# Induced attention and a maxout layer in one kernel: another list of work, some products in column tiles, another head

## The chip, the cores and the metric

One NeuronCore of a Trainium2 chip runs the whole program. The metric is device time in microseconds (us) of one execution, median of the runs shown. The profile is of one further execution, whose own time stands beside its span below.

## What is computed

```python
def mab(q, kv):                       # scale = 1 / sqrt(128)
    a = softmax(scale * q @ kv.T); return a @ kv
h = mab(inducing, x)                  # x: 4 x 12544 x 128, inducing: 32 x 128
y = mab(x, h)                         # 4 x 12544 x 128
g = maximum(y @ w1, y @ w2)           # w1, w2: 128 x 1024
out = g @ w_out                       # 50176 x 128, f32
```

The kernel uses maximum(a, b) = a + relu(b - a): the ReLU part goes through 1024 hidden columns, the linear part y @ w1 @ w_out through one 128 x 128 matrix. Since y is a weighted sum of the 32 rows of h, y @ (w2 - w1) is e @ (h @ (w2 - w1)), where e are the 32 weights of a token before division by their sum (`hwd` is h @ (w2 - w1), `m1` is h @ w1 @ w_out). The division comes last, when a result leaves PSUM.

## The kernel before

Each batch has 98 chunks of 128 tokens. Chunks stand in 27 blocks of up to 4 quarters x 4 chunks: quarter q of a block has its 32 rows of e on partitions 32q to 32q + 31.

Work on TensorE has three tilings. **Full array**: a final product (L932) has 128 x 128 ReLU values as the stationary operand and streams 128 columns of w_out; 8 of them, and the linear part, make a chunk of output, and up to 4 chunks share a PSUM bank (a group). **Row tiles**, 32 x 128: a phase (L1031, products at L1085) runs up to four quarters side by side, 512 columns each, hwd times e, into a bank for each; with fewer than four quarters the linear part of a group (e times m1, same line) may be one of them. **Column tiles**, 128 x 32: `stage` (L657) makes four quarters' scores, whose exp (ScalarE, L669) is e of a block; `pool_scores` (L356) and `pool_accum` (L414) are the first attention of batches 1 to 3.

A bank of a phase is emptied by ScalarE (L1102) or VectorE (L1105) with a ReLU into the quarter's buffer (two of 4096 columns for each quarter). A finished group is divided on its way out of PSUM by VectorE (L964) or ScalarE (L971), after the digit of its index in `EVICT`, and SP stores it. `turn_e2` (L720, L724) has GpSimd add up e and take the reciprocals.

The order of work in the steady part is a string, `ORDER` (L1113): a number is so many final products; `pN.M` a phase of N quarters; `s` a stage; `c`, `t`, `a`, `r` pooling scores, DMA transpose, sums, rest; `x` a DMA transpose of x; `g` a block's denominators; `e`, `h`, `w`, `m` the small products of a batch; `H`, `W` parts of the weights. The engine of a ReLU is the one that would end first by a planner (`Clock`, L21) that runs beside the program's writing; a bit of M turns that choice over. The planner also fills long waits with idle products (`keep_busy`), and picks banks.

Before that stands the **head**: batch 0 arrives in 12 parts (part 0 by SP in f32, the others by GpSimd's DMA queue, which casts to f16 on the way; L195), then the weights in four pieces (L253, L254) and w_out (L255). Each part is transposed by TensorE in two halves (L276; copied out by VectorE, L280, and ScalarE, L283), gives scores (L292), exp (L305), and the sums of e (L319) and e times x (L328). The order is the string `HEAD` (L814), with the due times of the parts in `LANDED`. At its end: the differences w2 - w1 (L573: 0 to 255 and 256 to 511 by VectorE, 512 to 1023 by GpSimd), casts of w1 (L579 by VectorE, L582 by ScalarE), hT4 (L473), two quarters of hwd (L521, evicted at L525), the first block's e (L684, L696), w1's transposes (L589, L596, L599) and w1 @ w_out (L607). `H1` is hwd's second half, evicted by VectorE, and the second half of the transposes; `W` is L607.

Of the kernel before, what the change touches and what calls it, by code (L numbers as in the profile page):

```python
# [9 lines left out]
F16 = mybir.dt.float16  # L10
# [10 lines left out]
class Clock:  # L21


    PAIR = 0.0558
    SWITCH = {"full": 0.11, "row": 0.097, "col": 0.097}
    LAT = 0.20
    ROW = 0.224
    SEM = 0.05

    def __init__(self):  # L30
        self.pe = self.act = self.dve = self.sp = 0.0
        self.pool = self.loading = self.loaded = 0.0
        self.stored = [0.0] * NOUT
        self.issue, self.tile = 0.0, [0.0] * 4
        self.mode = "full"
        self.bank = [0.0] * 8
        self.idle = {}
        self.log = []
        self.busy = {}
# [7 lines left out]
    def run(self, us, mode="full", ready=0.0, why="data"):  # L47
        if mode != self.mode:
            self.pe += self.SWITCH[mode]
            self.busy["sw"] = self.busy.get("sw", 0) + self.SWITCH[mode]  # L50
# [6 lines left out]
    def on_act(self, ready, us, tail=0.12):  # L57
# [3 lines left out]
    def on_dve(self, ready, us, tail=0.085):  # L61
# [3 lines left out]
    def on_sp(self, ready, us=1.33):  # L65
# [9 lines left out]
        return max(start + us + 2.4, late)  # L75
# [56 lines left out]
def kernel(  # L132
# [28 lines left out]
    relup = ctx.enter_context(tc.tile_pool(name="relup", bufs=2))  # L161
    outp = ctx.enter_context(tc.tile_pool(name="outp", bufs=NOUT))
# [7 lines left out]
    uid = [0]  # L170

    def bank(shape, dtype=F32, only=None):
        i = min(range(8), key=lambda j: ck.bank[j]) if only is None else only
        uid[0] += 1
        return i, psum.tile(shape, dtype, name=f"ps{uid[0]}", tag=f"bank{i}", bufs=1)
# [7 lines left out]
    parts[0] = [(0, 14), (14, 14), (28, 14), (42, 14), (56, 7), (63, 7), (70, 7), (77, 7), (84, 6), (90, 4), (94, 2), (96, 2)]  # L183
# [6 lines left out]
    def load_x(b, i, after=None):  # L190
# [5 lines left out]
        if b:  # L196
# [3 lines left out]
            st[b]["ld", i] = ck.loaded = ck.pe + 8.0 + 2.75 * i if b > 1 else 26.2 + 2.5 * i  # L200
# [13 lines left out]
    head16 = relup.tile([128, 4096], F16, name="head", tag="relu3")  # L214
# [10 lines left out]
    wf = relup.tile([128, 4096], F16, name="wf", tag="relu0").bitcast(F32)  # L225
    w1f, w2f = wf[:, 0:J], wf[:, J : 2 * J]
    w1s = relup.tile([128, 4096], F16, name="w1s", tag="relu1")
# [10 lines left out]
    with tc.manual_schedule(engines={ET.PE, ET.DVE, ET.Activation, ET.Pool, ET.SP}):  # L238

        xf = relup.tile([128, 4096], F16, name="xf", tag="relu2")[:, 0 : 256 * P1].bitcast(F32)  # L240
        xf = xf.rearrange("p (k c) -> p k c", c=C)
# [3 lines left out]
        load_x(0, 1)  # L245
        make_identity(nc, identity16)
        load_x(0, 2)
        make_identity(nc, identity32)
        for i in range(3, len(parts[0])):
            load_x(0, i)  # L250
        for h in range(2):
            sl = slice(512 * h, 512 * (h + 1))
            nc.gpsimd.dma_start(out=w1f[:, sl], in_=moe_w1[:, sl])  # L253
            nc.gpsimd.dma_start(out=w2f[:, sl], in_=moe_w2[:, sl])  # L254
        nc.gpsimd.dma_start(out=woutp, in_=moe_w_out.rearrange("(jb j) c -> j jb c", j=128))  # L255
# [6 lines left out]
        nc.gpsimd.memset(m1bd, 0.0)  # L262
# [3 lines left out]
        LANDED = [0.0, 7.58, 9.72, 11.95, 13.05, 14.12, 16.27, 17.37, 18.31, 18.94, 19.26, 19.57]  # L266

        def p1_transpose(b, i, half):
            k0, n = parts[b][i]
            xn = xn_at[b, i]  # L270
            h = min(8, (n + 2) // 2)
            g, m = ((0, h), (h, n - h))[half]
            assert m
# [3 lines left out]
            end = ck.run(0.0555 * m, ready=max(ck.bank[bi], LANDED[i] + 0.1), why="T")  # L277
            dst = xT_tiles[b % 2][:, k0 + g : k0 + g + m, :]
            if half == 0:
# [7 lines left out]
        def p1_scores(b, i):  # L287
# [12 lines left out]
            if n > 2:  # L300
                et = etp.tile([128, P1, M], F16, name=f"et_{b}_{i}", tag="et")
            else:
                at = 1024 + 2 * M * (i % 2)
                et = head16[:, at : at + 2 * M].rearrange("p (k m) -> p k m", m=M)
            nc.scalar.activation(out=et[:, 0:n, :], in_=ps[:, 0 : n * M], func=AF.Exp, scale=scale)  # L305
            ck.bank[bi] = ck.on_act(end, 0.05 + n * M / 1200.0)
            st[b]["et", i] = et, ck.bank[bi]

        def p1_accum(b, i, lo=0, hi=P1):
# [4 lines left out]
            if b == 0:  # L314
                last = i == len(parts[0]) - 1
                ck.wait(ready, "p1")
                for j in range(lo, hi, 4):
                    m = min(4, hi - j)
                    nc.tensor.matmul(  # L319
                        out=st[0]["eps"][0 : m * M, 0:1],  # L320
                        lhsT=et[:, j : j + m, :].rearrange("p k m -> p (k m)"),
# [880 lines left out]
```

## Time and profile before

| | before |
|---|---|
| median of 3 runs | 318.08 us (318.03 to 318.1) |
| the profiled execution | 317.76 us, its span 316.0 us |
| granted TensorE clock | 0.998 |
| first phase of the steady part | 23.44 us |
| last product of TensorE ends | about 312.9 us |
| DMA | 55.81 MB, mean 177 GB/s |

In the profile PE is TensorE, PEld its loads of stationary operands, DVE VectorE, ACT ScalarE, POOL GpSimd. The span goes from the first to the last instruction. A group of instructions is named by its line, engine, operation and operands, then the count, the busy time (of all, in us), the mean of one in ns, and the idle time before them with what ended it. A wait is written "who <- whom: us in total, times, longest". The chain leads from the last instruction back to what released each; its rows are the start, the us, and what ran. Products on TensorE overlap in the pipeline and their shown ends are modelled, so their pace is the difference of starts.

### The profile page before, as it was taken

What the parts mean: (1) busy time and instruction counts of PE and PEld (TensorE: products, weight loads), DVE (VectorE), ACT (ScalarE), POOL (GpSimd) and SP (SyncE); (2) the same over time, 40 slices, a digit from 0 to 9 for tenths busy, and PEclk for the clock granted to TensorE, in tenths of its full rate; (3) what the DMA queues carried; (4) which work ended last, traced back from release to release, by engine and by line L of the source; (5) the groups of instructions that cost most, each with busy time, mean ns of one, the idle gap of its engine ahead of it and who ended that gap; (6) DMA issues with size and microseconds to landing.
All of it is one profiled execution on the core that took longest, in us unless ns stands there. A gap on an engine that the chain in (4) does not pass through costs nothing.

```text
span 316.0 us, 12577 instructions
## 1 busy us (share of the span) xinstructions
PE 308.6 (98%) x5308; PEld 239.9 (76%) x5308; DVE 274.5 (87%) x488; ACT 280.2 (89%) x580; POOL 125.8 (40%) x187
## 2 busy tenths in 40 slices
PE   6998999999999999999999999999999999999996
PEld 3885777777877777778877787887868777788885
DVE  2468999999878999988999899989899889999885
ACT  3669999999999999998999989899999999998891
POOL 7363060666620066067510064674406564461500
PEclk9999999999999999999999999999999999999999
DMA  8999999989799999898499999897323233324232
GB/s 203 208 252 205 207 219 146 207 229 230 127 218 245 245 183 174 190 233 207 121 225 252 213 227 215 204 174 203 106 85 118 100 106 118 119 88 140 102 120 101
DMA packets 81336, 55.81 MB, mean 177 GB/s; under 512 B 62816, under 2 KB 66176, under 8 KB 81280
## 3 DMA queue, kind: packets, MB, share of 16 engines
q1 hardware_dynamic: 75312, 41.32, 55.8%
q0 software_dynamic: 5968, 13.70, 22.4%
q8 instruction: 41, 0.67, 0.9%
q14 instruction: 15, 0.12, 0.1%
HBM read 27.28 MB, written 25.69 MB: 168 GB/s over the span
## 4 chain that ended last, share of the span: by engine, by line
PE 94%; DMA 2%; ACT 1%; DVE 1%; issue 1%; POOL 0%; POOLq 0%
PE ps L932 60%; PE ps L1085 23%; DMA xn<-in_x_dram 2%; PE ps L657 2%; PE ps L356 2%; PE ps L414 2%; PE ps L276 1%; PE ps L328 1%; PE ps L292 1%; PE ps L521 0%; DVE relu L1105 0%; PE ps L319 0%; ACT e L669 0%; DVE o L964 0%; ACT e_first L696 0%
## 5 line engine op out<-in xcount | busy, mean ns | idle before, releaser
L1102 ACT ACTIVATE relu<-ps 128x512 f16<-128x512 f32 x470 | 241.0, 627 | 17.5 <-PE ps L1085 16.5
L1105 DVE TENSOR_SCALAR relu<-ps 128x512 f16<-128x512 f32 x314 | 199.7, 684 | 20.6 <-PE ps L1085 19.0
L932 PE MATMUL ps<-woutp,relu 128*128 128x128 f16 x3136 | 203.5, 219 | 0.2
L932 PEld LDWEIGHTS <-relu 128*128 128x128 f16 x3136 | 176.6, 98 | 34.4 <-issue 28.7
L1085 PE MATMUL ps<-e,hwd 32*128 32x512 f16 (+2 forms) x840 | 82.8, 361 | 0.1
L720 POOL TENSOR_TENSOR half<-ed 128x256 f32<-128x256 f16 (+2 forms) x23 | 14.1, 613 | 145.8 <-DMA ed<-e 145.8
L724 POOL TENSOR_TENSOR rd<-den,minus 128x16 f32<-128x16 f32 (+2 forms) x23 | 60.7, 2639 | 1.8
L964 DVE TENSOR_TENSOR o<-ps,rd 128x512 f32<-128x512 f32 (+3 forms) x83 | 53.2, 643 | 3.9 <-PE ps L1085 2.8
L1085 PE MATMUL ps<-m,e 32*128 32x128 f16 x372 | 36.8, 216 | 0.0
L1085 PEld LDWEIGHTS <-hwd 32*128 32x128 f16 x880 | 26.7, 91 | 12.8 <-issue 3.8
L1085 PEld LDWEIGHTS <-e 32*128 32x128 f16 x372 | 22.4, 92 | 10.4 <-issue 2.7
L720 POOL TENSOR_TENSOR half<-half 128x32 f32<-128x32 f32 (+3 forms) x69 | 22.3, 323 | 5.4
L195 POOL DMA_DIRECT2D xn<-in_x_dram x32 | 17.6, 563 | 5.7 <-DMA xn<-in_x_dram 4.3
L280 DVE COPY xT<-ps 128x512 f16<-128x512 f16 (+3 forms) x12 | 5.7, 485 | 8.6 <-PE ps L276 8.6
L964 DVE TENSOR_TENSOR o<-ps,rp 128x512 f32<-128x512 f32 (+3 forms) x20 | 12.8, 642 | 0.0
L369 ACT ACTIVATE eu<-ps 128x512 f16<-128x512 f32 x18 | 11.0, 617 | 0.6 <-PE ps L356 0.3
L669 ACT ACTIVATE e<-ps 128x512 f16<-128x512 f32 (+2 forms) x21 | 11.1, 607 | 0.3 <-PE ps L657 0.2
L283 ACT COPY xT<-ps 128x768 f16<-128x768 f16 (+3 forms) x10 | 5.7, 574 | 4.3 <-PE ps L276 4.2
L276 PE MATMUL ps<-identity,xn 128*128 128x128 f16 x98 | 7.6, 220 | 1.4 <-DMA xn<-in_x_dram 0.9
L657 PE MATMUL ps<-xT,hT 128*32 128x512 f16 (+3 forms) x110 | 8.1, 361 | 0.1
L276 PEld LDWEIGHTS <-xn 128*128 128x128 f16 x98 | 5.5, 97 | 2.9 <-DMA xn<-in_x_dram 1.2
L356 PE MATMUL ps<-xT,inducingT 128*32 128x512 f16 x72 | 6.8, 386 | 0.0
(110 smaller groups left out, 117.7 us busy)
## 6 DMA issues: line engine op xcount, KB each, us to landing
out_dram<-o SPq DMA_DIRECT2D x90, 256.0 KB, 3.0
xn<-in_x_dram POOLq DMA_DIRECT2D x24, 448.0 KB, 10.4
out_dram<-o SPq DMA_DIRECT2D x10, 128.0 KB, 2.9
wf<-in_moe_w_dram POOLq DMA_DIRECT2D x4, 256.0 KB, 6.0
xn<-in_x_dram POOLq DMA_DIRECT2D x4, 224.0 KB, 10.2
xT<-xn SPq DMA_TRANSPOSE x33, 4.4
xf<-in_x_dram SPq DMA_DIRECT2D x1, 512.0 KB, 3.7
xf<-in_x_dram SPq DMA_DIRECT2D x1, 384.0 KB, 4.2
```

The source lines that it names most:

```text
L195: nc.gpsimd.dma_start(out=xn_at[b, i][:, 0:n, :], in_=xr[b, :, k0 : k0 + n, :])
L276: nc.tensor.transpose(ps[:, j, :], xn[:, g + j, :], identity16)
L356: nc.tensor.matmul(out=ps[32 * g : 32 * (g + 1), :], lhsT=inducingT, rhs=xT_tiles[b % 2][:, U * u + 4 * g : U * u + 4 * (g + 1), :], start ...
L657: nc.tensor.matmul(out=ps[32 * q : 32 * (q + 1), 128 * t : 128 * (t + n)], lhsT=hq, rhs=xT[:, c : c + n, :], start=True, stop=True, tile_p ...
L669: nc.scalar.activation(out=blk.e2[:, 0 : 128 * wd], in_=ps[:, 0 : 128 * wd], func=AF.Exp, scale=st[0]["rs"] if blk.b == 0 else scale,)
L720: nc.gpsimd.tensor_tensor(out=dst, in0=cur[:, :, 0:n], in1=cur[:, :, n : 2 * n], op=ALU.add)
L724: nc.gpsimd.tensor_tensor(out=rp[:, 0:wd, :].rearrange("p t q -> p (t q)"), in0=den[:, 0 : 4 * wd], in1=minus1[:, 0 : 4 * wd], op=ALU.pow,)
L932: nc.tensor.matmul(out=g.ps[:, 128 * c : 128 * (c + 1)], lhsT=g.blk.relu[g.q][:, 128 * (jb * w4 + t) : 128 * (jb * w4 + t + 1)], rhs=woutp ...
L964: nc.vector.tensor_mul(osb[:, 0:m, :], g.ps[:, 0 : m * C].rearrange("p (s c) -> p s c", s=m), g.blk.rp[:, t0 : t0 + m, q : q + 1].broadcas ...
L1085: nc.tensor.matmul(**seq.pop(0))
L1102: nc.scalar.activation(out=dst, in_=src, func=AF.Relu)
L1105: nc.vector.tensor_scalar(out=dst, in0=src, scalar1=0.0, scalar2=None, op0=ALU.max)
```

## The change

- `ORDER` is another list. The bits of `pN.M` now say outright which evictions VectorE makes; the planner chooses none.
- New words: `nK` is K final products, each cut into four products of 32 stationary columns in column tiles. `V` is both halves of w1's transposes, `H0` hwd's second half evicted by ScalarE, without transposes.
- `EVICT`: three more of the last six groups leave by ScalarE, the last among them.
- Head: 13 parts, the second and third of 7 chunks each. Six parts (2 to 7) arrive in f32 and are cast by VectorE (first half) and GpSimd (second half); GpSimd issues a further load after each cast. Another order (`HEAD`). Columns 256 to 511 of the difference and the second cast of w1 go to GpSimd. The sums of e are always over four chunks.
- PSUM is one tile cut into banks; the ReLU buffers are one tile for each quarter, the output buffers one tile. Who reads and writes them in turn stays.
- The planner's constants change (products, changes of tiling, lags), and it counts how fast TensorE is fed with instructions.

```diff
-    parts[0] = [(0, 14), (14, 14), (28, 14), (42, 14), (56, 7), (63, 7), (70, 7), (77, 7), (84, 6), (90, 4), (94, 2), (96, 2)]
+    parts[0] = [(0, 14), (14, 7), (21, 7), (28, 14), (42, 14), (56, 7), (63, 7), (70, 7), (77, 7), (84, 6), (90, 4)]
+    parts[0] += [(94, 2), (96, 2)]
...
+        homes = {0: (2, 0, 0, 14), 2: (0, 1, 0, 7), 3: (1, 1, 0, 14), 4: (2, 1, 0, 14)}
+        homes.update({5: (0, 1, 7, 7), 6: (3, 1, 0, 7), 7: (3, 1, 7, 7)})
...
-        LANDED = [0.0, 7.58, 9.72, 11.95, 13.05, 14.12, 16.27, 17.37, 18.31, 18.94, 19.26, 19.57]
+        LANDED = [0.0, 6.54, 7.56, 9.57, 11.58, 12.6, 13.62, 15.69, 16.79, 17.74, 18.4, 18.76, 19.11]
...
+        def cast_x(i):
+            for half, (g, m) in enumerate(cut(parts[0][i][1])):
+                eng = nc.gpsimd if half else nc.vector
+                eng.tensor_copy(out=xn_at[0, i][:, g : g + m, :], in_=wide[i][:, g : g + m, :])
...
+            load_next()
...
         HEAD = """
-        1a 1b I S0 2a 2b S1 A0 S2 3a 3b A1 4a 4b S3 S4 A2 A3 5a 5b A4 6a 6b S5 7a 7b S6 A5 8a 8b S7
-        A6 9a 9b 10a S8 11a N S9 S10 A7 S11 A8 A9 A10 A11
+        1a 1b 0b C2 I 2b 2a S0 C3 S1 C4 S2 A0 A2 C5 3b A1 3ax 4a 4b S3 5b C6 5a 6a S4 C7 A3 S5 6b A4 L
+        7ax 7bx S6 A5 8bx 8a 9a 9b S7 A6 10bx 10a 11ax S9 12a N S8 S10 A7 S11 S12 A9 A8 A10 A11 A12
         """
...
+        load_x(1, 0)
+        difference(nc.vector, 0, 256, 20.45, 0.34)
+        difference(nc.gpsimd, 256, 512, 20.45, 0.64)
+        load_x(1, 1)
+        load_x(1, 2)
+        difference(nc.gpsimd, 512, J, 22.35, 1.25)
+        cast_w1(1)
...
+            tiles = [(32 * i, 32 * (i + 1)) for i in range(4)] if narrow else [(0, 128)]
+            for lo, hi in tiles:
+                nc.tensor.matmul(
+                    out=g.ps[lo:hi, 128 * c : 128 * (c + 1)],
+                    lhsT=relu[:, lo:hi],
+                    rhs=woutp[:, jb, :],
...
+                    tile_position=(0, lo) if narrow else None,
...
+        def relu_out(q, blk, unit, bi, ready, vector):
...
+            if vector:
+                nc.vector.tensor_scalar(out=dst, in0=src, scalar1=0.0, scalar2=None, op0=ALU.max)
...
+            else:
+                nc.scalar.activation(out=dst, in_=src, func=AF.Relu)
...
         ORDER = """
+        s p4.11 p2.1 s H0 V W p4.2 2 m0 p1 n10 p2.3 p2 9 p3.1 14 p2.1 p3.2 n11 p4.3 16 p4.12 1 g2 p2 19
+        x1.0 p4.2 12 p4.3 14 p2.1 p3.2 16 p2.2 p3.4 14 x1.1 p4.4 13 p3.7 s x1.2 s n7 s n7 x1.3 p4.12 3
+        x1.4 x1.5 13 g3 p4.8 4 x1.6 3 x1.7 6 p4.5 15 p2 2 p3.5 x1.8 12 p4.12 n9 s c1.0 n6 x1.9 n3 p1
+        p4.10 14 p4.9 13 p4.2 15 g4 10 p4.1 p3.5 27 p2.2 p3.4 14 p4.5 n7 c1.1 n3 p3.1 15 p4.10 c1.2 x1.10
+        n9 c1.3 t1.1 n7 p4.5 14 p4.12 21 p3.1 p3.1 19 t1.3 3 p4.10 c1.4 g5 n10 p3.4 12 p4.2 22 p2.1 p4.9
+        n13 c1.5 7 r1 a1.1 p4.2 p3.3 19 a1.3 p4.2 t1.5 p2.1 29 p4.4 p3.6 25 g6 p4.8 n7 a1.5 p2 p3.1 1 e1
+        12 p4.1 h1 18 m1 w1 s s s s p3.3 31 p3.1 p4.4 31 p3.2 g1 p3.4 24 p3.2 p3.1 2 x2.0 25 p3.3 p4.2 20
+        p4.6 x2.1 p2 n17 s x2.2 p4.12 19 p3.6 p2 23 p3.5 p4.2 27 p1 p4.6 s n14 p4.2 18 p4.3 2 x2.3 12
+        x2.4 g9 p4.7 6 p3 14 p3.4 x2.5 12 p4.12 17 p4.5 x2.6 n5 x2.7 c2.0 n9 p1 p4.10 x2.8 24 p3.2 x2.9
+        p3.4 22 p2.1 p3.3 n7 s c2.1 g10 n9 p4.8 15 p4.9 16 c2.2 p3.1 p3.1 27 p3.1 t2.1 p3.2 26 x2.10 p3.2
+        p3.3 n14 g11 c2.3 p4.10 17 t2.3 p4.4 18 p3.4 p3.2 n18 a2.1 c2.4 p3.4 p3.6 23 p4.3 19 p4.3 g12 p2
+        31 p4.3 p3.1 19 r2 1 c2.5 a2.3 n6 p4 p2.3 t2.5 32 p4.3 p3.4 31 p2.1 g13 p4.8 n11 a2.5 p4.8 17 e2
+        p3.2 6 p4.12 6 h2 20 p3.6 p3 14 w2 m2 13 p4.14 s n3 x3.0 s s n11 p3.1 p2.1 13 s p4.12 2 x3.1 13
+        p2.1 p3.2 22 p3.2 p3.5 25 p3 x3.2 x3.3 p4.12 28 p3.1 10 p3.2 p3.4 27 p3.4 p3.4 22 p4.3 n6 x3.4 s
+        s n8 p2.1 p3.4 8 g16 19 p4.1 p3.3 37 p4.1 x3.5 p3.6 36 p4 x3.6 p3.7 21 c3.0 p3.1 3 g17 13 p4.9 s
+        c3.1 n16 p1 p4.6 x3.7 24 p3.2 p3.4 21 p2.2 p3.2 3 t3.1 15 x3.8 p1 p4.9 21 p3.6 p3.4 21 g18 1 g15
+        p2 p4.12 31 x3.9 g7 p3.1 x3.10 p4.3 23 c3.2 a3.1 c3.3 p2.1 p4.6 22 p4.2 19 p2.1 t3.3 p4.8 27 p4.9
+        g19 p2 31 p4.8 p3.5 13 r3 a3.3 n4 c3.4 c3.5 p4.3 20 t3.5 p4.2 p2.1 20 p4.12 13 p2.1 p3.2 29 p4.6
+        g20 p3.6 28 a3.5 p4.5 p2 5 e3 23 h3 4 p4.11 p3 15 w3 13 s p4.8 2 m3 18 p2.1 g21 p3.4 14 p3.5 s g8
+        n3 s n10 s n3 p3.6 p3 22 p4.9 p1 26 p4.3 p3.2 22 p2.2 g22 p2 22 p4.4 p3.1 24 p3.7 s n7 s n8 p3.2
+        p3.1 29 p3.6 p4.4 20 p4.4 19 p2.2 g23 p4.4 30 p4.1 p3.6 20 s n5 p2.1 p3.4 11 p4.5 21 p4.5 p2 22
+        p3.6 p2 15 p3.5 g24 p2 13 p4.2 19 p4.4 p1.1 n11 p4.9 21 p3.6 p3 29 g14 p4.5 p3.2 19 p4.5 17 p4.4
+        g25 14 p4.9 22 p3 p3.6 28 p2.2 p3.4 22 p4 p2.3 22 p2.2 p4.1 g26 24 p3.5 p2 27 p4.6 p3.4 38 p4.12
+        p3.2 32 p4.9 g27 p2 22 p2.2 p3.4 23 p3.6 p4.4 38 p3.6 p3 19 p4.3 22 p2.1 p3.2 31 p4.15 p4.6 64
         """
...
-        EVICT = "000000000000000000000000101000000000000000000000010000000000000000000010000000000000000000000000000000010000"
+        EVICT = "000000000000000000000000101000000000000000000000010000000000000000000010000000000000000000000000000000011011"
```

More of the change, by code (lines that the diff above doesn't have):

```diff
@@ L276, in p1_transpose @@
                 nc.tensor.transpose(ps[:, j, :], xn[:, g + j, :], identity16)
-            end = ck.run(0.0555 * m, ready=max(ck.bank[bi], LANDED[i] + 0.1), why="T")
+            end = ck.run(0.0555 * m, ready=max(ck.bank[bi], st[0].get(("cast", i, half), LANDED[i] + 0.1)), why="T")
             dst = xT_tiles[b % 2][:, k0 + g : k0 + g + m, :]
-            if half == 0:
+            if (half == 0) != other:
                 nc.vector.tensor_copy(out=dst, in_=ps[:, 0:m, :])
@@ L885, in keep_busy @@
                 return
-            turn = ck.SWITCH["full"] if ck.mode != "full" else 0.0
+            turn = ck.SWITCH[ck.mode]["full"] if ck.mode != "full" else 0.0
             n = int((until - ck.pe - turn - 0.1) / 0.11)
@@ L1078, in phase @@
                 ]])
+            ran = sum(len(seq) for _, _, _, seq in parts_)
             while any(seq for _, _, _, seq in parts_):
```

326 lines of the change are left out of this document (172 added, 154 removed).

## The prediction

> **What bounds the kernel now.** I read the page from the top, then the chain, then the waits, then the timeline of TensorE.
>
> ```profile
> span 316.0 us, 12577 instructions
> ...
> PE 308.6 (98%) x5308; PEld 239.9 (76%) x5308; DVE 274.5 (87%) x488; ACT 280.2 (89%) x580; POOL 125.8 (40%) x187
> ...
> PEclk9999999999999999999999999999999999999999
> ...
> PE 94%; DMA 2%; ACT 1%; DVE 1%; issue 1%; POOL 0%; POOLq 0%
> ```
>
> TensorE is 94% of the chain, at full clock. ScalarE and VectorE are nearly as busy (89% and 87%), so the next question is who waits for whom. In the waits and in the groups by line (count, busy us, mean ns of one, idle before):
>
> ```profile
> DVE relu L1105 <- PE ps L1085: 19.0, 57, 0.9
> ACT relu L1102 <- PE ps L1085: 16.5, 46, 0.9
> ...
> PE ps L607 <- ACT w1s L599: 1.0, 1, 1.0
> ...
> PE ps L276 <- DMA xn<-in_x_dram: 0.9, 2, 0.8
> ```
> ```profile
> L1102 ACT ACTIVATE relu<-ps 128x512 f16<-128x512 f32 x470 | 241.0, 627 | 17.5 <-PE ps L1085 16.5
> L932 PE MATMUL ps<-woutp,relu 128*128 128x128 f16 x3136 | 203.5, 219 | 0.2
> L1105 DVE TENSOR_SCALAR relu<-ps 128x512 f16<-128x512 f32 x314 | 199.7, 684 | 20.6 <-PE ps L1085 19.0 <-ACT relu L1102 0.6
> ```
>
> The two evicting engines wait for TensorE (19.0 and 16.5 us), not the reverse. TensorE's idle column (0.2) hides waits shorter than a product's 219 ns, so its pace is read from start to start. The chain near the end (start, us, what), and the timeline:
>
> ```profile
> 299.93 2.34 PE ps L932 x40
> 302.27 0.55 PE ps L1085 x9
> 302.82 1.28 PE ps L932 x21
> ```
> ```profile
> 108.78 0.40 PE L1085 MATMUL ps<-e,hwd 32*128 32x512 f16 x4
> 109.11 0.95 PE L932 MATMUL ps<-woutp,relu 128*128 128x128 f16 x14
> ```
>
> Nineteen more final products cost 2.34 - 1.28 = 1.06 us: 55.8 ns each, which leaves 2.34 - 40 x 0.0558 = 0.11 us for a change of tiling. A visit to row tiles lasts 0.33 us with one phase (108.78 to 109.11) and 0.55 with two: 0.22 a phase, and 0.11 for the other change. So 3136 x 55.8 ns = 175 us is fixed, and the list of work can only save changes of tiling, phases and waits inside them. The waits look like this (stretch, its us, busy us of L1085 alone):
>
> ```profile
> 28.31:29.01 0.70, 0.70 (x11) 0.42 (x11) 1.00 1.04 205
> 43.98:44.42 0.44, 0.44 (x4) 0.10 (x4) 1.00 1.03 391
> 45.37:45.86 0.49, 0.49 (x4) 0.18 (x4) 1.00 0.67 33
> 308.09:308.68 0.59, 0.59 (x21) 0.47 (x21) 1.00 0.00 0
> ```
>
> The second and third are single phases that took 0.44 and 0.49 instead of 0.33. I went through all 151 visits to row tiles from start to start: 33, of which the first and last rows above are the first and last, are over their 0.33 or 0.55 by more than 0.04 us, and together by 2.9 us. That is what a better list can win inside the visits.
>
> **The list itself, by counting its words.** Before, 151 visits to row tiles, 151 to the full array, 33 to column tiles: 335 runs; 250 phases. After, 157, 136 and 36: 329 runs; 249 phases. Six changes at 0.11 and one phase at 0.22: -0.66 and **-0.9 us** together. The mask bits put 319 ReLU evictions on VectorE where L1105 has 314; five move by their own 0.68 us to an engine that waits 19.0 us for TensorE: nothing, and 0.68 x 5 = 3.4 us if that cover were gone. The new buffers (one PSUM tile, one tile for each quarter's ReLU, one for the outputs) keep the same readers ahead of the same writers, slice by slice: nothing on TensorE; at worst waits on engines whose idle time is in those two rows.
>
> **The products in column tiles.** 314 of 3136 final products become four of 32 columns. Only the pooling shows such tiles with 128 columns streamed:
>
> ```profile
> 205.05 0.40 PE L356 MATMUL ps<-xT,inducingT 128*32 128x512 f16 x4
> 205.28 0.62 PE L414 MATMUL ps<-xn,eT 128*32 128x128 f16 x32
> 205.73 0.39 PE L356 MATMUL ps<-xT,inducingT 128*32 128x512 f16 x4
> 206.05 0.60 PE L1085 MATMUL ps<-e,hwd 32*128 32x512 f16 x5
> ```
>
> From 205.28 to 205.73 run 32 products: 14.1 ns each, 56.3 ns for four, against 55.8 for one whole. So 314 x 0.5 ns = **+0.15 us**, as long as TensorE is fed that fast. This whole run is 40 products, in 1.00 us = 0.45 + 2 x 0.22 + 0.11, with no stretch; no longer one exists in this trace. In the new list 23 column runs are longer (up to 108), with 564 products beyond their fortieth. The nearest slower row is the head's:
>
> ```profile
> 15.53 0.52 PE L328 MATMUL ps<-et,xn 128*128 128x32 f16 x14
> 15.90 0.27 PE L276 MATMUL ps<-identity,xn 128*128 128x128 f16 x2
> ```
>
> 14 products in 0.37 us, 26 ns each. So the unknown lies between 0 and 564 x (26 - 14) = +6.8 us; below nothing it can't be, since the same sums are streamed. I take the first, whose tiles and shape are these.
>
> A rule speaks against the change here: the Trainium skill ("TensorE: Matmul & The Clock Gate", section "Wait — 56ns, not 53.3ns?") says that starts are never closer than about 25 ns. By it every split product would take 100 ns and the sum would be 314 x 44 ns = 13.9 us worse, near 330. The 14.1 ns of this trace contradict it for products in different column tiles.
>
> **The waits inside the visits** (2.9 us): no row says how many a new order with a fixed engine for each eviction keeps. All (0) or none (-2.9) are the ends; I take a third, **-1.0 us**, because a visit waits for a bank that one of two engines at 87-89% has yet to empty, and their totals hardly change.
>
> **The head.** What ends last before the steady part is a chain on ScalarE:
>
> ```profile
> 23.41 0.51 ACT w1s L582
> 23.91 0.59 ACT e L669
> 24.50 0.49 ACT relu L1102
> ...
> 25.56 0.48 ACT w1s L599
> ...
> 26.09 0.40 PE ps L607 x4
> ```
>
> The cast of w1 (0.51) goes to GpSimd. In its place comes the ReLU of p2.1 (0.49), and the H0 that follows has hwd's second half evicted by ScalarE (about 0.5, estimated from its L1102 pitch of 0.49) where VectorE did it. The chain to L607 is 0.5 us longer, with two more units (0.22) done by then: +0.3. Against it stands what begins it. DMA in 40 slices of the first 26 us:
>
> ```profile
> GB/s 0 0 76 88 290 408 408 297 225 219 199 226 215 204 215 204 226 188 201 210 210 235 188 206 205 197 194 266 402 405 416 262 102 194 196 174 220 187 210 213
> ```
>
> Casting loads write about 208 GB/s of halves, so read about 416; plain loads write 402 to 416. So the six parts that now land in f32 come no sooner by this row; the list's due times say 0.46 earlier. What helps more is that the first part of GpSimd's queue is halved: the 0.9 us in which L276 waited for loads (two times, in the rows of waits above) is waiting for the first whole parts. From 0 to -1.2 I take -0.6, between the two. Head: **-0.3 us**, from -0.9 to +0.5. The new casts cost nothing if they keep up with the loads; see the second rival. The difference of columns 256 to 511 leaves VectorE (0.42) for GpSimd, beside TensorE's sums.
>
> **The tail.** After TensorE's last product the last chunk is scaled by VectorE in 0.29 us; now by ScalarE:
>
> ```profile
> 312.97 0.29 DVE o L964
> ```
> ```profile
> L971 ACT ACTIVATE o<-ps,rd 128x128 f32<-128x128 f32 x11 | 3.4, 376 | 0.4 <-PE ps L1085 0.2
> ```
>
> 376 ns: **+0.1 us**. The other two groups that move end before it.
>
> **Sum**: -0.9 + 0.15 - 1.0 - 0.3 + 0.1 = -1.9 us. The profiled execution took 317.76 us around its span of 316.0, 0.3 under the median of 318.08; 1.9 below the median is **316.2 us**.
>
> **Rivals.**
> First, **starved column runs** (the other side). Past the forty products shown, TensorE's instructions arrive no faster than 26 ns a product, +6.8 us: 323.0. It decides from 1.9 + 0.64 = 2.5 us over 564 products, 4.5 ns each: slower from 18.6 ns on. For: a split product needs four times the instructions, in runs up to 108. Against: forty go unstretched. Chance 0.10.
>
> Second, **late weights**. GpSimd now casts halves of six parts before it issues the last loads:
>
> ```profile
> 3.61 3.30 POOL L195 DMA_DIRECT2D xn<-in_x_dram  x6
> ```
> ```profile
> L573 POOL TENSOR_TENSOR w<-wf 128x512 f16<-128x512 f32 x1 | 1.3, 1269 | 1.4 <-DMA wf<-in_moe_w_dram 1.4
> ...
> L784 DVE CAST xn<-xf 128x1024 f16<-128x1024 f32 x1 | 0.7, 700 | 2.9 <-DMA xf<-in_x_dram 2.9
> ```
> ```profile
> 17.61 0.54 POOL L254 DMA_DIRECT2D wf<-in_moe_w_dram  x1 [0.44 <-DMA xn<-in_x_dram]
> ...
> 22.97 1.27 POOL L573 TENSOR_TENSOR w<-wf 128x512 f16<-128x512 f32 x1 [1.45 <-DMA wf<-in_moe_w_dram]
> ```
>
> 24 tiles of 128 columns at L573's 2.5 ns a column are 7.6 us, and six issues at 0.55 make 10.9; from 7.56 us, the new list's due time for the first of these parts, that ends near 18.4, so the last weights would be issued some 1.3 us after the 17.61 of now, and the difference that waits for them (1.45) with them: 317.5. If VectorE's casts of those parts (32 tiles at 0.70 a 1024 columns, 2.8 us) also shut GpSimd out, 320.3. Half of L573's price, for one input in place of two, ends it in time. Chance 0.10, half of it slower.
> The Trainium skill ("SBUF — State Buffer", section "SBUF: two separate sides") has the lock: VectorE in a two-port mode and GpSimd exclude one another for a whole instruction. The row of six issues disagrees as far as it goes: 0.55 each, the same as elsewhere, though the 0.70 us cast of L784 ran among them; casts on both at once no row here shows.
>
> Third, **the list wins nothing**: other visits wait as long, and what is counted goes into the head: 317.2 to 318.2. For: the totals of the two evicting engines stay. Chance 0.20, half of it within 0.2%.
>
> Fourth, **all waits go** and the head gives its 0.9: 1.9 + 0.6 more, 313.7. Chance 0.15.
>
> The forecast itself, 315.1 to 317.2, has 0.45.
>
> **How the numbers follow.** 0.2% is 0.64 us, about what a measurement of this kernel tells from no change. Faster: 0.45 + 0.15 + 0.08 of the third + 0.01 of the second = 0.69. Same: 0.10 + 0.03 = 0.13. Slower: 0.10 + 0.06 + 0.02 = 0.18. The range 313.4 to 319.0 leaves out the first rival, the worst of the second and a third of the fourth.
>
> **What would show it.** In the profile after: column runs of L932's successor at 56 ns for four, also late in a run of seventy (else the first rival); about 249 phases and visits of 0.33 and 0.55, with fewer than 33 long ones (else the third); the last weight loads issued by 17.6 and L607's successor near 26 us; the first phase before 23.44. The forecast is wrong if ReLU evictions stop waiting for TensorE and TensorE begins to wait for them.

## The result and the profile after

The changed kernel takes **329.05 us** (median of 4 executions, 327.38 to 330.64), the kernel before on the same chip 318.05: a ratio of 1.0351, 95% interval 1.0328 to 1.0374. Forecast were 316.2 and a range to 319.0: the sign was wrong. The profiled execution took 328.05 us with a span of 326.2. In the experiments below a time is the median of all executions, while a ratio (to the kernel before, run beside it) and its 95% interval leave out executions more than 1.5% over the fastest of their kernel, two of which took 700 us (one in `before_x_early`, one in `before_no_x23`). In the changed kernel `o` is called `osbs`, the PSUM tile `psall`; L995 holds the final products (L932 before), L1170 the phases in row tiles (L1085), L1030 the scaling of outputs on VectorE (L964), L1055 their stores (L989), L227 the transposes of x by DMA (L208), L214 the loads of x (L195), L213 the pacing copy (L194), L774 and L778 the turn of e on GpSimd (L720, L724).

The page of the changed kernel: span, the first row of busy times, the clock by slices, the chain by engine.

```profile
span 326.2 us, 14490 instructions
...
PE 310.0 (95%) x6251; PEld 242.2 (74%) x6251; DVE 278.1 (85%) x498; ACT 280.5 (86%) x584; POOL 127.9 (39%) x190
...
PEclk9999999999999979999999989999999999999999
...
PE 80%; DMA 12%; DVE 4%; POOL 1%; issue 1%; ACT 0%; ACTq 0%; DVEq 0%; POOLq 0%
```

TensorE's share of the chain fell from 94% to 80%, DMA's rose from 2% to 12%, and the clock has two dents. The waits name the DMA:

```profile
DVE osbs L1030 <- DMA out_dram<-osbs: 7.7, 2, 3.9
...
PE psall L710 <- DVE osbs L1030: 3.4, 1, 3.4
...
PE psall L1170 <- DVE osbs L1030: 3.1, 1, 3.1
```

Twice VectorE waits 3.9 us for a store to give an output buffer back, and each time TensorE then waits for VectorE. Before, the only such wait was 0.4 us. When the n-th final product starts (from the timeline of TensorE, four split products counted as one), in us:

| n | 1 | 400 | 800 | 1000 | 1400 | 1600 | 2400 | 3000 | TensorE's end | span |
|---|---|---|---|---|---|---|---|---|---|---|
| before | 27.08 | 66.15 | 105.92 | 124.04 | 161.69 | 179.92 | 252.24 | 302.05 | 312.93 | 315.99 |
| after | 28.19 | 66.47 | 105.69 | 128.83 | 165.93 | 189.25 | 261.81 | 311.63 | 322.51 | 326.19 |
| after - before | +1.11 | +0.32 | -0.23 | +4.79 | +4.24 | +9.33 | +9.57 | +9.58 | +9.58 | +10.2 |

The head loses 1.1 us, the steady part wins that back and more by the 800th product, and two places lose 5 us each. Between and behind them next to nothing is lost (+0.25 us from the 1600th product to the end). Here they are (stretch; its us; busy us of PE, PEld, DVE, ACT, POOL; clock; DMA share; GB/s):

```profile
112.00:114.00 2.00, 0.00 (x0) 0.00 (x0) 0.00 (x0) 0.30 (x1) 0.00 (x0) 1.00 0.73 227
114.00:116.00 2.00, 1.03 (x7) 0.30 (x7) 1.97 (x4) 0.10 (x1) 0.00 (x0) 0.87 1.21 326
116.00:118.00 2.00, 2.00 (x22) 1.59 (x21) 2.00 (x4) 1.30 (x3) 0.00 (x0) 0.50 1.08 394
...
184.00:186.00 2.00, 0.00 (x0) 0.00 (x0) 0.67 (x2) 0.00 (x0) 0.00 (x0) 1.00 1.11 341
186.00:188.00 2.00, 1.92 (x50) 1.10 (x49) 1.76 (x5) 1.38 (x3) 0.00 (x0) 0.79 1.26 115
188.00:190.00 2.00, 2.00 (x23) 2.00 (x20) 1.35 (x3) 1.28 (x3) 0.00 (x0) 0.50 1.17 311
```

TensorE and VectorE stand still together, and afterwards TensorE is granted half its clock for a while. In its timeline 14 final products take 0.96 us ahead of the stop and 1.67 behind it:

```profile
110.72 0.96 PE L995 MATMUL psall<-woutp,relus 128*128 128x128 f16 x14
114.77 0.39 PE L1170 MATMUL psall<-e,hwd 32*128 32x512 f16 x3 [3.10 <-DVE osbs L1030]
...
117.09 1.67 PE L995 MATMUL psall<-woutp,relus 128*128 128x128 f16 x14
```

That is how a wait of 3.1 us costs 5. The Trainium skill ("TensorE: Matmul & The Clock Gate", section "What's actually happening") says that an idle window of about 3.4 us puts the array back to half clock; the two waits of 3.1 and 3.4 us, each followed by 3.4 us at 0.50, are close to that, but in `before_both` below a wait of 2.8 us was enough, while one of 1.8 us was not.

What held the store? SyncE's queue in the changed kernel, and then in the kernel before (start, us, what):

```profile
95.92 1.43 SPq L227 DMA_TRANSPOSE xT<-xn  x1
97.59 2.62 SPq L1055 DMA_DIRECT2D out_dram<-osbs  x2
100.26 9.79 SPq L227 DMA_TRANSPOSE xT<-xn  x1
110.14 0.53 SPq L1055 DMA_DIRECT2D out_dram<-osbs  x1
...
170.59 10.76 SPq L227 DMA_TRANSPOSE xT<-xn  x1
```
```profile
95.22 9.98 SPq L989 DMA_DIRECT2D out_dram<-o  x6
...
108.30 5.78 SPq L208 DMA_TRANSPOSE xT<-xn  x4
```

In the changed list x2.0 and x2.1 come at 95.9 and 100.3 us, and the issue of the second holds the queue for 9.8 us; before, the queue sent six stores in that time and the first transposes of that batch only at 108.3. The store sent behind x2.0 is in the chain of waits, and VectorE waits for it:

```profile
97.59 16.35 DMA out_dram<-osbs
```
```profile
114.03 0.69 DVE L1030 TENSOR_TENSOR osbs<-psall,rp 128x512 f32<-128x512 f32 x1 [3.93 <-DMA out_dram<-osbs]
```

It took 16.35 us to land. It was issued ahead of x2.1, so it isn't the 9.8 us of that issue that held it, but x2.0 in front of it: x2.0 landed at 113.38 us, the store at 113.93. At the second stop it is the same (x3.0 landed at 184.64, the store behind it at 185.21), and in the traces of all runs the DMAs that SyncE issued after 60 us landed in the order of their issue. The stores of the kernel before that were issued from 86 to 107 us, among its loads, took 9.3 at most:

```profile
DMA to landing us min/median/max: 3.7/8.1/9.3
```
And why are these transposes slow? They run among the loads of x. GpSimd's queue, changed kernel, then before:

```profile
86.75 0.42 POOL L774 TENSOR_TENSOR half<-ed 128x128 f32<-128x128 f16 x1 [2.65 <-DMA ed<-e]
...
88.56 1.65 POOL L778 TENSOR_TENSOR rd<-den,minus 128x8 f32<-128x8 f32 x1
90.16 0.18 POOL L213 COPY pace<-hacc 128x1 f32<-128x1 f32 x1
90.28 3.82 POOL L214 DMA_DIRECT2D xn<-in_x_dram  x7
```
```profile
78.71 0.43 POOL L720 TENSOR_TENSOR half<-ed 128x128 f32<-128x128 f16 x1 [0.31 <-DMA ed<-e]
...
84.34 0.18 POOL L194 COPY pace<-hacc 128x1 f32<-128x1 f32 x1 [2.18 <-DVE hacc L447]
84.84 3.81 POOL L195 DMA_DIRECT2D xn<-in_x_dram  x7 [0.31 <-PE ps L932]
```

GpSimd works its queue in order. In the new list the word g6 (a turn of e) stands ahead of the loads and itself waits for a DMA, so the loads go out at 90.3 instead of 84.8; in the next batch, behind g13, at 163.3 instead of 155.2. From then on the loads take some 22 us, and the last lands at 113.0 (before at 107.0). So before, x2.0 came 23.5 us after the loads' issue, behind them; now 5.6 us after it, in their midst. x3.0 went from 15.0 to 5.2 us, where the loads took 22.0 us (before) and 21.0. The time from issue to landing of the 33 transposes, before and after:

```profile
DMA to landing us min/median/max: 2.9/4.4/8.5
```
```profile
DMA to landing us min/median/max: 3.0/4.6/17.5
```

The four first transposes of the two batches are the long ones: 17.5, 14.8, 16.1 and 15.6 us. What they wait for can be read from the landings: the last load ahead of x2.0 landed at 113.03 us and x2.0 at 113.38, the last load ahead of x3.0 at 184.37 and x3.0 at 184.64. In the traces of all runs below, and of both kernels, 83 DMA transposes were issued after 60 us while loads issued ahead of them were still under way. None landed before the last of these loads did, and the 17 that had been issued 14 us or more ahead of that landing came 0.3 to 0.6 us behind it. So a transpose among the loads takes what is left of the loads, and so does a store behind it. Plain stores among the loads, with no transpose ahead of them, don't wait so: eight of the kernel before landed ahead of loads issued before them. The Trainium skill ("Advanced Engine Details and Errata", section "X-Bar Transpose (TRN2)") says that such transposes are as fast as regular DMAs; the median of 4.6 doesn't speak against that, the ones among the loads do (14.8 us and more, where stores among loads took 9.3 at most).

### The profile page after: what moved, and what is told of

Read it like the earlier page. It is cut to its first block, busy times and chain, and to the rows that moved or that the text cites. A ratio compares the mean times of both kernels' runs of the same rounds, so it can differ in the third digit from the quotient of the medians.

```text
span 326.2 us, 14490 instructions
## 1 busy us (share of the span) xinstructions
PE 310.0 (95%) x6251; PEld 242.2 (74%) x6251; DVE 278.1 (85%) x498; ACT 280.5 (86%) x584; POOL 127.9 (39%) x190
## 4 chain that ended last, share of the span: by engine, by line
PE 80%; DMA 12%; DVE 4%; POOL 1%; issue 1%; ACT 0%; ACTq 0%; DVEq 0%; POOLq 0%
PE psall L995 52%; PE psall L1170 20%; DMA out_dram<-osbs 10%; DMA relus<-in_x_dram 3%; DVE relus L1107 2%; PE psall L710 2%; PE psall L411 1%; PE psall L470 1%; DVE osbs L1030 1%; PE psall L318 1%; POOL xn L307 1%; PE psall L383 1%; PE psall L578 1%; PE psall L334 0%; POOL relus L280 0%
## 5 line engine op out<-in xcount | busy, mean ns | idle before, releaser
L1110 ACT ACTIVATE relus<-psall 128x512 f16<-128x512 f32 x460 | 236.5, 618 | 25.2 <-PE psall L1170 24.2
L1107 DVE TENSOR_SCALAR relus<-psall 128x512 f16<-128x512 f32 x316 | 200.6, 683 | 21.8 <-PE psall L1170 20.6
L995 PE MATMUL psall<-woutp,relus 128*128 128x128 f16 (+1 forms) x4046 | 207.5, 220 | 0.3 <-DVE m L617 0.2
L995 PEld LDWEIGHTS <-relus 128*128 128x128 f16 (+1 forms) x4046 | 179.1, 98 | 35.7 <-issue 29.0
L1170 PE MATMUL psall<-e,hwd 32*128 32x512 f16 (+2 forms) x840 | 83.3, 364 | 3.3 <-DVE osbs L1030 3.1
L774 POOL TENSOR_TENSOR half<-ed 128x256 f32<-128x256 f16 (+2 forms) x22 | 13.4, 611 | 172.4 <-DMA ed<-e 172.4
L778 POOL TENSOR_TENSOR rd<-den,minus 128x16 f32<-128x16 f32 (+2 forms) x22 | 57.8, 2627 | 1.7
L1030 DVE TENSOR_TENSOR osbs<-psall,rd 128x512 f32<-128x512 f32 (+2 forms) x76 | 49.0, 647 | 5.5 <-DMA out_dram<-osbs 3.8
L1170 PE MATMUL psall<-m,e 32*128 32x128 f16 x372 | 37.5, 218 | 0.0
L1170 PEld LDWEIGHTS <-hwd 32*128 32x128 f16 x880 | 27.1, 91 | 13.8 <-issue 4.9
L1170 PEld LDWEIGHTS <-e 32*128 32x128 f16 x372 | 22.6, 93 | 10.7 <-issue 2.4
L774 POOL TENSOR_TENSOR half<-half 128x64 f32<-128x64 f32 (+4 forms) x66 | 21.3, 323 | 5.2
L1030 DVE TENSOR_TENSOR osbs<-psall,rp 128x512 f32<-128x512 f32 (+3 forms) x24 | 15.6, 650 | 5.1 <-DMA out_dram<-osbs 3.9
L723 ACT ACTIVATE e<-psall 128x512 f16<-128x512 f32 (+2 forms) x21 | 11.1, 597 | 3.1 <-PE psall L710 3.1
L214 POOL DMA_DIRECT2D xn<-in_x_dram x21 | 11.5, 564 | 0.0
```

The lines of the kernel that those rows point to most:

```text
L214: nc.gpsimd.dma_start(out=xn_at[b, i][:, 0:n, :], in_=xr[b, :, k0 : k0 + n, :])
L723: nc.scalar.activation(out=blk.e2[:, 0 : 128 * wd], in_=ps[:, 0 : 128 * wd], func=AF.Exp, scale=st[0]["rs"] if blk.b == 0 else scale,)
L774: nc.gpsimd.tensor_tensor(out=dst, in0=cur[:, :, 0:n], in1=cur[:, :, n : 2 * n], op=ALU.add)
L778: nc.gpsimd.tensor_tensor(out=rp[:, 0:wd, :].rearrange("p t q -> p (t q)"), in0=den[:, 0 : 4 * wd], in1=minus1[:, 0 : 4 * wd], op=ALU.pow,)
L995: nc.tensor.matmul(out=g.ps[lo:hi, 128 * c : 128 * (c + 1)], lhsT=relu[:, lo:hi], rhs=woutp[:, jb, :], start=not g.started, stop=(state["m ...
L1030: nc.vector.tensor_mul(osb[:, 0:m, :], g.ps[:, 0 : m * C].rearrange("p (s c) -> p s c", s=m), g.blk.rp[:, t0 : t0 + m, q : q + 1].broadcas ...
```

## The experiments

**The theory**: the placement of words in the list that occupy other queues than TensorE's: x words (SyncE) too soon, g words (GpSimd) ahead of the loads. **The rivals**: the split products; the new head and merged buffers; the evictions' engines; the new order of products itself.

**Remove the x transposes from among the loads** (`x_late`, in the changed kernel):

```diff
-  p3.1 2 x2.0 25 ... p4.6 x2.1 p2 n17 s x2.2 p4.12 ... p4.3 2 x2.3
+  p3.1 2 25 ... p4.6 p2 n17 s p4.12 ... p4.3 2 x2.0 x2.1 x2.2 x2.3
-  n3 x3.0 s s ... p4.12 2 x3.1 13 ... p3 x3.2 x3.3
+  n3 s s ... p4.12 2 13 ... p3 x3.0 x3.1 x3.2 x3.3
```

> The changed kernel, with only five words of its list moved: the first three transposes of x of batch 2 stand beside the fourth, and the first two of batch 3 beside the third, so that all are issued when the loads of their batch are nearly in. Theory (transposes issued among the loads hold up the output stores behind them in SP's queue, six output buffers run out, VectorE and then TensorE stop): both stops of 3.3 and 3.6 us and the half clock behind them go, 317.5 to 320. Rival one (the split products are what costs): 327 to 330. Rival two (merging PSUM, ReLU and output buffers into single tiles adds waits): 327 to 330.

324.03 us, ratio 1.0209 (1.0176 to 1.0242), over the theory's 317.5 to 320: nearly half the loss back, not all. Both stops are gone, and a new wait stands in their place, the first pooling scores for the transposes:

```profile
PE psall L411 <- DMA xT<-xn: 3.2, 5, 1.2
```

**Run the split products whole** (`no_split`: `narrow = False`).

> The changed kernel with all 314 split products run whole on the full array, the list otherwise as it is. Theory: the stops stay, about 45 more changes of tiling at 0.1 us come in, 328 to 334. Rival one (split products): 322 or less. Rival two (merged tiles): 328 to 334.

333.25 us (1.042, 1.0397 to 1.0443): as the theory expected, the stops stay (5.4 and 3.1 us of TensorE). The split products aren't the cause.

**Move x words early in the kernel before** (`before_x_early`: x2.0, x2.1, x3.0, x3.1 to places like those of the new list).

> The kernel before, with only four words of its list moved: the first two transposes of x of batches 2 and 3 about as early after their loads as the changed kernel has them. Theory: a stop of 2 to 4 us in each of the two batches with a half clock behind it, 322 to 329. Rivals one and two: 318, as before, since no product is split and no tile merged.

318.65 us (1.0029, 1.0007 to 1.0051). A miss. The transposes held the queue (5.3 and 8.2 us, the slowest landed after 15.2), and the slowest store took 9.4 us in the first of the two batches and 12.4 in the second, but no engine stopped: the loads here had left 5.3 and 7.7 us sooner than in the changed kernel, and the last landed at 106.6 and 176.5. An early transpose alone doesn't do it.

**More output buffers** (`nout11`: `NOUT` 6 to 11, paid for with `NXN` 12 to 9).

> The changed kernel with 11 output buffers in place of 6 (and 9 buffers for x in place of 12, to make room, which no batch needs at once). Theory: 11 groups at 2.7 us last 30 us, longer than the 16 us for which a store is held up, so the stops go though the transposes are as late as ever in landing: 318 to 321. Rival one: 327 to 330. Rival two, if the wait is for the single output tile and not for the buffer in it: 327 to 330.

324.32 us (1.0218, 1.0173 to 1.0263), over the theory's 318 to 321. The transpose still holds the queue for 10.7 us, yet no one waits for a store any more: the buffers are what joins the slow store to TensorE. What remains is again 3.7 us of waits of the scores for x, so the late transposes cost by two ways, and a repair of one leaves the other.

**The turn of e ahead of the loads.** In the changed kernel g6 and g13 earlier (`g_early`), then with the old `EVICT` (`g_early_evict`), then with whole products (`g_early_no_split`):

```diff
-  n13 c1.5 7 r1 a1.1 ... 25 g6 p4.8 n7 a1.5
+  g6 n13 c1.5 7 r1 a1.1 ... 25 p4.8 n7 a1.5
-  p3.1 19 r2 1 c2.5 ... p2.1 g13 p4.8 n11 a2.5
+  p3.1 g13 19 r2 1 c2.5 ... p2.1 p4.8 n11 a2.5
```

> The changed kernel with two words of its list moved: g6 from just before a1.5 to before c1.5, and g13 from just before a2.5 to before r2, as far ahead as the kernel before has them. Theory (GpSimd runs its work in order; the sums of g6 and g13 stand ahead of the next batch's loads and wait for a DMA transpose, so the loads go out 5 us later after the sums of the pooling than in the kernel before, and everything that needs them, transposes, stores behind them and the first pooling scores, is late): pace copy near 85 and 158 us, no stop of TensorE over 1 us in the steady part, 317.5 to 320.5. Rival (the early transposes of x alone hold the stores up, whenever the loads start): the stops stay, 325 to 330. Rival (the whole list is too tight for the loads): 322 to 326, with waits at the pooling scores.

> As the run with g6 and g13 moved, and the engines of the last output groups as before (only one of the last six by ScalarE). Theory: from TensorE's last product to the end it takes 3.7 us in the changed kernel and 3.06 in the kernel before because of ScalarE's evictions; 0.6 us less than the run with the two words moved alone. Rival (the stores at the end are late for other reasons): no difference.

> As the run with g6 and g13 moved, with all 314 split products run whole. Theory (split products cost what whole ones cost and save changes of tiling; some 45 changes more at 0.1 us): 3 to 6 us above the run with the two words moved alone. Rival (they save nothing, since the list before had as few changes without them): within 1 us of it.

323.0 (1.0123, 1.006 to 1.0185), 323.42 (1.0091, 1.0059 to 1.0123) and 321.53 us (1.0134, 1.0085 to 1.0183): more than half the loss back in each, all over the 317.5 to 320.5 expected of the first, and no difference among the three that the intervals tell. In the first the pacing copy came at 91.8 us all the same, held now by g5, which waited 7.67 us for its DMA, in an execution that was 2.8 us behind the changed kernel's by the 400th product, after half clock from 27.7 to 34.5 us; but in the second batch at 159.7 instead of 163.2; in the third at 85.8 and 156.2, with no stop of TensorE over 0.45 us behind the head. That whole products would be slower there was a miss.

**The same in the kernel before** (`before_g_late`: g6 and g13 to just before a1.5 and a2.5).

> The kernel before with only g6 and g13 moved to just before a1.5 and a2.5, as the changed kernel has them. Theory: the pace copies at 84.3 and 154.7 us come some 3 to 5 us later, and the loads with them; its first transposes stand later in the list, so the stores are not held up, but the first pooling scores of batches 2 and 3 wait: 319 to 324. Rival: 318, no change.

320.75 us (1.0099, 1.0066 to 1.0131), as expected: the copy at 91.34 and 160.37 (7.0 and 5.7 us later, more than expected), and the scores wait 1.5 us for x.

**Both moves in the kernel before**, everything else as it was (`before_both`).

> The kernel before with both moves at once and nothing else: g6 and g13 go to just before a1.5 and a2.5, so that the next batch's loads stand behind the turn of e, and the first transposes of x of the last two batches (x2.0, x2.1, x3.0, x3.1) go early. Alone the first gave +2.7 us and the second +0.6 us. Theory (a transpose of x that is issued among the loads lands late, the output stores behind it in SyncE's queue land late, and the output buffers run out): together they make what neither makes alone, stops of 2 to 4 us of TensorE near 112 and 182 us on output buffers, each with a lapse of the clock; 324 to 330 us. Rival (the stops need the new list's order of products, the two moves only add): 321 to 322 us and no wait of VectorE for a store of over 1 us.

**327.02 us** against 317.86 (1.0286, 1.0234 to 1.0337): +9.2 us from six words moved, where each half alone gave +0.8 and +2.8 against the kernel before run beside it (+0.6 and +2.7 against its first runs). Both stops are there. Its waits, and SyncE's queue:

```profile
DVE o L964 <- DMA out_dram<-o: 6.5, 3, 3.5
PE ps L657 <- DVE o L964: 2.8, 1, 2.8
...
PE ps L1085 <- DVE o L964: 2.2, 2, 1.8
```
```profile
100.45 9.54 SPq L208 DMA_TRANSPOSE xT<-xn  x1
...
168.23 10.95 SPq L208 DMA_TRANSPOSE xT<-xn  x1
```

The old order of products, whole, with the old head and buffers, stops on output buffers at the same places: 1.8 us up to 114.9, without a lapse of the clock, and 2.8 us up to 184.0, with one of 3.4 us. Its 1000th product starts 3.0 us late, its 1600th 7.3.

**The list alone** (`list_only`: the changed list, splits, engines and planner on the old head and buffers), and the same with g5, g6, g12, g13 earlier, x words late and the old `EVICT` (`list_fixed`).

> The kernel before with the changed kernel's list, its split products, its engine for each eviction and its planner, but with the head and the separate buffers of the kernel before. Theory (the list puts g5, g6 and g12, g13 late, the next loads behind them in GpSimd's queue, and the transposes of x among those loads): the stops of the changed kernel are here too, 324 to 330. Rival (new head, half clock after its waits, merged buffers): 316 to 319.

> The run with the new list under the old head, with nine words of that list moved (g5, g6, g12, g13 earlier; the first transposes of x of batches 2 and 3 later) and the old engines for the last groups. Theory: loads out before 86 and 157 us, no stop over 0.6 us, the six changes of tiling and shorter waits inside the visits are left over: 316 to 318. Rival (the list is too tight elsewhere): 319 or more.

333.33 us (1.0488, 1.0439 to 1.0536), over the theory's 324 to 330, with stops of 3.7 us each: neither the new head nor the merged buffers are needed. The repaired list: 325.21 (1.021, 1.0181 to 1.0238), over its 316 to 318 by 7. It has no long stop, but its profiled execution is 2.9 us behind the kernel before by the 400th product, after half clock from 28.8 to 35.6 us, and 7.0 by the 1600th; of that, four single waits explain some (0.5 to 0.8 us, two of them for e). Words moved by hand took the long stops away and not the whole loss.

**All nine words moved in the changed kernel, with the old `EVICT`** (`all_early`).

> The changed kernel with the same nine words moved and the old engines for the last groups, under its own head. Theory: as the run with the old head plus what the new head costs, 0.5 to 1 us, and some 3 us more in executions in which the clock halves behind the waits near 25 us: 317 to 321. Rival (the new head is free): equal to the run with the old head.

324.88 us (1.0223, 1.0177 to 1.0269), a miss of the same kind: three waits of 0.9 to 1.2 us for xT and eT from 65 us on.

**The loads sooner instead of the words**: in `pool_accum`, five of the seven loads at the fourth sum (`load_soon`), and the same with the x words late (`load_soon_x_late`).

```diff
+            if u == 3 and b + 1 < B:
+                for i in range(5):
+                    load_x(b + 1, i, acc[:, 0:1] if i == 0 else None)
...
-                for i in range(7):
-                    load_x(b + 1, i, acc[:, C : C + 1] if i == 0 else None)
+                for i in range(5, 7):
+                    load_x(b + 1, i, acc[:, C : C + 1] if i == 5 else None)
```

> The changed kernel with its list as it is; only the pacing copy and the loads of the next batch's first five parts are issued earlier, with the fourth sum of the pooling and not behind the last one, so that they stand ahead of the late turns of e in GpSimd's queue. Theory (loads too late for the transposes' place): the loads go out several us sooner than 90.3 and 163.3 us, the first transposes of x stand among them for a shorter time, no wait of VectorE for a store over 1 us, and 317 to 321 us. Rival (the place of the x words alone is at fault, whatever the loads do): both stops stay, 326 to 330 us.

> The same earlier loads, and x2.0 to x2.2 and x3.0, x3.1 moved behind, beside x2.3 and x3.2, where the moved words alone gave 324.0 us with the first pooling scores waiting for the transposes. Theory: with the loads sooner the transposes are sooner too and those waits shrink; 317 to 319 us, about the kernel before or a little under. Rival (late transposes cost the scores whatever the loads do): 322 to 325 us.

With the list untouched the stops go: no wait of VectorE for a store, and in SyncE's queue the transpose that took 9.8 us takes 4.5.

```profile
83.65 0.18 POOL L213 COPY pace<-hacc 128x1 f32<-128x1 f32 x1
83.78 2.76 POOL L214 DMA_DIRECT2D xn<-in_x_dram  x5
```
```profile
101.41 4.45 SPq L227 DMA_TRANSPOSE xT<-xn  x1
```

The profiled execution took 319.2 us, at full clock until TensorE's end, where the theory had 317 to 321; the median is 323.28 (1.0135, 1.0106 to 1.0165), over it, with a mean clock of 0.978 to 0.999 by execution. With the x words late as well it is 326.87 (1.0239, 1.0175 to 1.0303): worse, over the theory and the rival. Its profiled execution (323.2) falls back by 3.7 us against that of `load_soon` between the 700th and the 1600th product, in single waits of at most 0.9 us; so the late place is no better than the early one once the loads are sooner, and why the other executions are longer still the runs don't show.

**Without the 22 transposes of x of the last two batches** in either kernel (this part of the computation is left out, and the scores there read old data): `after_no_x23`, `before_no_x23`.

> The changed kernel without the 22 DMA transposes of x of batches 2 and 3: part of the computation is left out, the two batches work on what stands in the transposed buffers from batches 0 and 1. Theory (all that the changed kernel loses in its steady part are waits for these transposes and for the stores behind them): no stop over 1 us after 30 us, 315 to 318. Rival (the list loses on the engines too): 320 or more.

> The kernel before with the same 22 transposes left out. Theory (they are already in time there): 317 to 318, so the changed kernel without them stands 0 to 2 us under it, which is what its list gains on TensorE. Rival: 315 or less, and the list gains nothing on TensorE either.

318.32 us (1.002, 0.9993 to 1.0047) and 318.68 (1.0019, 1.0003 to 1.0035). The kernel before gains nothing, the changed one 10.7 us: all that it had lost, it loses with these transposes in its list, and in the list before they cost nothing.

**The tail and the head.** `tail_only` is the kernel before with the changed `EVICT`. `w_later` is the changed kernel with the word W behind the next final products (`V p4.2 2 W m0`).

> The kernel before with only the engines of the last output groups changed as in the changed kernel (four of the last six by ScalarE). Theory (3.7 us from TensorE's last product to the end in place of 3.06 come from there): 318.5 to 318.8. Rival (the stores at the end come late for other reasons): 318.0.

> The changed kernel with one word moved: W (w1 @ w_out) behind the next phase and its two products. Theory (the 1.3 us wait ahead of W is what lets the clock halve near 27 us in some executions): that wait shrinks below 0.6 us, no half clock between 24 and 40 us; the stops of the steady part stay, so 326 to 330 all the same. Rival (the wait only moves): first final products no sooner.

317.99 us (1.0003, 0.9993 to 1.0012): the moved evictions cost nothing. `w_later`: 333.33 (1.0464, 1.039 to 1.0538), a miss: the wait (1.1 us) only went to the next reader, and half clock came into the head from 29.7 to 36.5 us.

## Why the prediction was wrong, step by step

- **What bounds the kernel** (TensorE, 94% of the chain): right of the kernel before. The step that failed is the sentence drawn from it, "the list of work can only save changes of tiling, phases and waits inside them". The list also says when x words enter SyncE's queue and g words GpSimd's, and I counted TensorE's words alone. What the runs showed in its place are two stops of TensorE, 3.1 and 3.4 us, on output buffers whose stores stood behind such a transpose: 10.1 us with the lapses of the clock. The kernel before had x2.0 23.5 us behind its loads; the new list put it 5.6 us behind them, which the two lists and the two queues' timelines of before would have let me estimate. Of a moved step the DMAs and the queues that it is moved past were to be counted, and weren't. No rival had SyncE's queue in it, so the 0.18 for slower stood for the wrong mechanisms. The sign that I had named for a wrong forecast didn't show either: the ReLU evictions waited for TensorE longer than before (20.6 and 24.2 us instead of 19.0 and 16.5).
- **Fewer changes and phases (-0.9), split products (+0.15), waits in visits (-1.0)**: together -1.75, and about right. Without the transposes of x the changed kernel runs from its first final product (28.44) to TensorE's end (312.77) in 284.33 us, where the kernel before takes 285.85: -1.5. The 33 long visits of the kernel before are together 3.35 us over their nominal time, not the 2.9 of the prediction; in the changed kernel 20 visits outside the half clock are over it by more than 0.04 us, together by 2.1.
- **Starved column runs** (the first rival): refuted. The longest run, 108 products:

```profile
140.74 1.19 PE L995 MATMUL psall<-woutp,relus 128*32 128x128 f16 x72
141.76 0.62 PE L470 MATMUL psall<-xn,eT 128*32 128x128 f16 x32
142.21 0.39 PE L411 MATMUL psall<-xT,inducingT 128*32 128x512 f16 x4
```

 72 products in 141.76 - 140.74 = 1.02 us are 14.2 ns each, also behind the fortieth.
- **The head (-0.3)**: wrong in sign. The first phase started at 23.76 (before 23.44), the first final product at 28.19 (27.08): +1.1. The chain to L607's successor, forecast near 26, ended at 27.19:

```profile
25.19 0.38 PE L578 MATMUL psall<-w,hT 128*128 128x512 f16 x1 [0.50 <-POOL w L625]
...
27.19 0.62 PE L660 MATMUL psall<-woutp,relus 128*128 128x128 f16 x8 [1.05 <-DVE relus L648]
```

 0.9 of the 1.1 us stand in the first row already (25.19; before 24.30). What is waited for (0.50) is the difference of columns 512 to 1023, which GpSimd made before as well. The second rival had the last weights issued some 1.3 us later, and they were (18.8, before 17.6), but they landed only 0.2 us later (23.0). The difference starts at 23.8 instead of 23.0 because GpSimd first makes the columns that came from VectorE (0.9 us) and issues two loads of x (1.1 us); so the 0.42 us moved off VectorE came back as a wait. The 1.05 stands where 0.98 stood before.
- **The tail (+0.1)**: from TensorE's end to the span's 3.68 us instead of 3.06, +0.6. It isn't `EVICT`, which alone costs nothing; with the changed `EVICT` the tail was also 3.24 us (`list_only`, `load_soon`), with the old one also 3.98 (`g_early_evict`). The cause stays open.
- **The third and fourth rivals** concerned the visits, which came out between: -1.2 of 3.35.

So of the +10.2 us between the two spans, 10.1 are the two stops with their lapses of the clock (-0.23 to +4.79 and +4.24 to +9.33 in the table), 1.1 the head and 0.6 the tail, against 1.6 won elsewhere. That the two moves of words suffice for 9.2 us is shown (`before_both`), that the transposes carry the loss too (`after_no_x23`), and that the output buffers join it to TensorE (`nout11`). Not shown is what holds a transpose until the loads ahead of it have landed.

## What to carry to other kernels

When a hand-written order of work changes, list for every queue, not only for the engine that bounds, which steps changed places, and for each DMA what was in flight at its old and its new time; here two shifts of 0.8 and 2.8 us together made 9.2. A queue that lands in order hands a slow transfer on to all that stands behind it, and the number of buffers says when the bounding engine notices: six output buffers hid a store of 12.4 us (`before_x_early`) and not one of 15.2. A wait of TensorE of about 3 us costs more than itself, through the clock behind it.

## What the runs showed of the chip that was not expected

- A DMA transpose issued among GpSimd's loads took 14.8 to 17.5 us to land (median of all 33: 4.6), held SyncE's queue 9.8 and 10.8 us (median 1.6), and a store between two of them landed after 16.35 us. None of the 83 that were issued among loads, in all runs, landed before the last load issued ahead of it.
- Products in column tiles start 14.2 ns apart in a run of 72, so that four cost what one whole product does (56 ns).
- Around each of the nine waits of TensorE of 2.8 to 5.4 us (in the changed kernel, `before_both`, `no_split`, `list_only` and `w_later`) the granted clock was 0.50 for 3.4 or 6.8 us. In `w_later` it was also 0.50 from 29.7 to 36.5 us, and the longest wait near it was 1.1 us, up to 28.7: a wait shorter than 3 us went ahead of a lapse there, while the wait of 1.05 us up to 27.2 in the changed kernel's profile was followed by none.
